# Layer 1's converted weights written over their raw high words, a PSUM bank of their own for the bits, and block 0's h in SBUF

## The chip, the cores and the metric

The kernel runs on one core of a Trainium2 chip. The metric is the device time of one execution in microseconds; the median of three runs of the kernel before is 961.95 us (960.44 to 962.39).

## What is computed

Strided and local attention over four batches of 576 tokens with eight heads, and then two dense feed-forward layers on all 2304 tokens. The weights come as float64. Cut to what matters:

```python
scores = scale * np.matmul(q, k.transpose(0, 1, 3, 2))
scores = np.where(masks[None, :, :, :], scores, -1000000000.0)
attn = np.exp(scores - np.max(scores, axis=-1, keepdims=True))
attn = attn / (np.sum(attn, axis=-1, keepdims=True) + 1e-09)
x = np.matmul(attn, v)            # then (2304, 512)
h = np.maximum(x @ w_in, 0.0)
x = h * h @ w_out                 # layer 1: 512 -> 2048 -> 512
h = x @ w_in2
P = a[0] + a[1] * h + a[2] * h**2 + a[3] * h**3
Q = 1.0 + np.abs(b[0]) * np.abs(h) + np.abs(b[1]) * h**2
out = (P / (Q + 1e-06)) @ w_out2  # layer 2
```

## The kernel before

The weights arrive as 64-bit floats, each as two 32-bit words. `to_f32` makes float32 of one half of a weight tile, 128 x 512 values: ACT takes the absolute value of the high word with a scale (L198, the tile `w32`, three buffers), VectorE shifts and masks it (L202), puts the sign in (L203) and the top bits of the low word (L204). For layer 1 the tile `bits` between these steps lies in PSUM, in the pool `psum` of eight banks that everything shares. `split_w` then rounds the float32 to fp32r for the high part `wh` (L220 on POOL, every fourth on ACT, L218) and subtracts for the low part `wl` (L221 on POOL, the first four on VectorE). A product of two float32 numbers is made of three fp32r matmuls: high by high, high by low, low by high.

The tokens are worked in six blocks of 384 (`NB`). A unit (j, f) of layer 1 is one of the 16 slices of 128 hidden columns for block j: `h_unit` runs 12 matmuls into one bank (L412), `act1` makes relu, square, the high part `gh` (L426) and the low part `gl` (L427), and `o_unit1`, two units later (`LAG`), runs 12 matmuls into the four banks of `acc` (L439). In block 0 h stays in its PSUM bank through all of `act1`: ACT does relu and square there, and VectorE makes `gl` from it. In later blocks relu goes to SBUF (L422), VectorE squares (L423) and POOL makes `gl`.

Attention runs in groups, two to a pair, woven into the units: scores (L285), maximum (L296), exponent (L309), row scale (L317, L318, L320), transposes (L327), values (L343), and the high and low parts of x (L368, L369). The groups of block 0 come first, then unit (0, 0) follows, and the groups of later blocks are spread over the units of the block before.

In block 0 the weights of layer 1 are converted just ahead of their use. `feed_w(3)` at the head of each unit converts three halves, in the order `wq`; 32 halves in all. The raw halves land in places that are free at that time (`homes`): the first 16 in tiles meant for later weights, the next 12 in eight of the same places again, and the last four in the staging pool; `load_raw` issues a load up to eight halves ahead, and a place that is used again waits until its earlier half has been read. In blocks 1 to 4 layer 2's weights are converted in the same way (`spill_w`) and written to DRAM.

The order of instructions on each engine is made by a scheduler at build time, by its own estimate of times and by the order in which the program text issues; at run time each engine keeps its order and waits on semaphores. TensorE, VectorE, ACT, POOL and the DMA queue of SP each have one.

Of the kernel before, what the change touches and what calls it, by code (L numbers as in the profile page):

```python
# [9 lines left out]
F32 = mybir.dt.float32  # L10
F32R = mybir.dt.float32r
I32 = mybir.dt.int32
BF16 = mybir.dt.bfloat16
AF = mybir.ActivationFunctionType
ALU = mybir.AluOpType
AX = mybir.AxisListType
PSUM = bass.MemoryType.PSUM

P = 128
# [3 lines left out]
DM, DFF = 512, 2048  # L23
NT = B * S
TB = 384
NB = NT // TB
NF = DFF // P
KT = DM // P
# [128 lines left out]
def moe_kernel(ctx, tc, qk, vp, w1, w2, a, b, masks, eye, out):  # L157
    nc = tc.nc
# [11 lines left out]
    gpool = ctx.enter_context(tc.tile_pool(name="gpool", bufs=1))  # L170
    first = ExitStack()
    stage = first.enter_context(tc.tile_pool(name="stage", bufs=3))
    psum = ctx.enter_context(tc.tile_pool(name="psum", bufs=8, space=PSUM))

    cst = cpool.tile([P, C_END], BF16, name="cst")
    ident = cpool.tile([P, P], F32, name="ident")
# [14 lines left out]
    def to_f32(layer, f, part, raw):  # L191

        lo, hi = raw[:, :, 0], raw[:, :, 1]
        w = stage.tile([P, DM], I32, tag="w32", bufs=3, name=f"w32_{layer}_{f}_{part}")
        wf = w.bitcast(F32)
        nc.scalar.activation(wf, hi.bitcast(F32), AF.Abs, scale=2.0**-112)  # L198
        bits = w
        if layer == 0:  # L200
            bits = psum.tile([P, DM], I32, tag="ps", name=f"bits{f}_{part}")
        nc.vector.tensor_scalar(bits, w, 3, 0x7FFFFFFF, ALU.logical_shift_left, ALU.bitwise_and)  # L202
        nc.vector.scalar_tensor_tensor(bits, hi, -0x80000000, bits, ALU.bitwise_and, ALU.bitwise_or)  # L203
        nc.vector.scalar_tensor_tensor(w, lo, 29, bits, ALU.logical_shift_right, ALU.bitwise_or)  # L204
        return wf

    def w_place(layer, f):
        wt[layer, f] = tuple(wpool.tile([P, 2 * DM], F32R, tag=f"w{c}{f}", name=f"w{c}{layer}_{f}") for c in "hl")
        return wt[layer, f]
# [3 lines left out]
    def split_w(wh, wl, wf):  # L213

        halves[0] += 1
        n = halves[0]
        if n % 4 == 0:
            nc.scalar.copy(wh, wf)  # L218
        else:
            nc.gpsimd.tensor_scalar(wh, wf, 1.0, 0.0, ALU.mult, ALU.add)  # L220
        (nc.vector if n <= 4 else nc.gpsimd).tensor_tensor(wl, wf, wh.bitcast(F32), ALU.subtract)  # L221
# [158 lines left out]
    def at_slot(n):  # L380

        load_groups(n + 4)
        if n < NG and n % 2 == 0:
            at_scores(n)
        if n < NG:
            at_max(n)
        if n == 2:
            warm_up(2)
        for m in range(max(0, n - 4), min(n, NG)):
            if n - m == lags(m)[1]:  # L390
                at_values(m)
        for m in range(max(0, n - 4), min(n, NG)):
            if n - m == lags(m)[0]:
                at_transpose(m)
        if n < NG:
            at_exp(n)
        for m in range(max(0, n - 4), min(n, NG)):
            if n - m == lags(m)[1]:
                at_out(m)
        if n < NG:  # L400
            at_norm(n)


    gt, acc = {}, {}

    def h_unit(layer, j, f, ps):
        xh, xl = xt[j]
        wh, wl = wt[layer, f]
        for kk in range(KT):
            c = slice(kk * P, (kk + 1) * P)  # L410
            for i, (w, x) in enumerate(((wh, xh), (wh, xl), (wl, xh))):
                nc.tensor.matmul(ps[:, :TB], w[:, c], x[:, kk, :], start=(kk == 0 and i == 0), stop=(kk == KT - 1 and i == 2))  # L412

    def act1(j, f, ps):
        psum_h = j == 0 or j == NB - 1 and f >= NF - EARLY
        if psum_h:
            nc.scalar.activation(ps[:, :TB], ps[:, :TB], AF.Relu)
            nc.scalar.activation(ps[:, :TB], ps[:, :TB], AF.Square)
            h = ps[:, :TB]
        else:  # L420
            h = gpool.tile([P, TB], F32, tag="r", name=f"r{j}_{f}", bufs=4)
            nc.scalar.activation(h, ps[:, :TB], AF.Relu)  # L422
            nc.vector.tensor_tensor(h, h, h, ALU.mult)  # L423
        gh = gpool.tile([P, TB], F32R, tag="gh", name=f"gh0_{j}_{f}", bufs=3)
        gl = gpool.tile([P, TB], F32R, tag="gl", name=f"gl0_{j}_{f}", bufs=3)
        last_act = nc.scalar.copy(gh, h).ins  # L426
        (nc.vector if psum_h else nc.gpsimd).tensor_tensor(gl, h, gh.bitcast(F32), ALU.subtract)  # L427
        gt[0, j, f] = gh, gl
        return last_act

    def o_unit1(j, f):
        if f == 0:
            acc[j] = [psum.tile([P, 512], F32, tag="ps", name=f"acc0_{j}_{e}") for e in range(KT)]
        gh, gl = gt.pop((0, j, f))
        wh, wl = wt[0, f]
        for e in range(KT):
            c = slice(DM + e * P, DM + (e + 1) * P)
            for i, (w, g) in enumerate(((wh, gh), (wh, gl), (wl, gh))):
                nc.tensor.matmul(acc[j][e][:, :TB], w[:, c], g, start=(f == 0 and i == 0), stop=(f == NF - 1 and i == 2))  # L439
# [39 lines left out]
    def load_raw(done):  # L479

        while len(raws) < min(len(wq), done + AHEAD):
            k = len(raws)
            place, free = homes[k]
            if slot < free or place and any(homes[i][0] == place for i in range(done, k)):
                break
            raws.append(load_w(0, *wq[k], place=place and "w" + place))
# [4 lines left out]
    def feed_w(n):  # L491
        for _ in range(n):
            load_raw(fed[0])
            if fed[0] < len(wq):
                f, part = wq[fed[0]]
                c = slice(part * DM, (part + 1) * DM)
                wh, wl = wt[0, f] if part else w_place(0, f)
                split_w(wh[:, c], wl[:, c], to_f32(0, f, part, raws[fed[0]]))
                fed[0] += 1
# [15 lines left out]
    def spill_w(f, part):  # L515

        wf = to_f32(1, f, part, load_w(1, f, part))
        parts = [stage.tile([P, DM], F32R, tag="w32", bufs=3, name=f"sp{c}{f}_{part}") for c in "hl"]
        split_w(*parts, wf)
        for z, t in enumerate(parts):  # L520
            nc.sync.dma_start(w2_dram[z, f][:, part * DM : (part + 1) * DM], t.bitcast(F32))
# [59 lines left out]
    NTT = TB // P  # L581

    def o_unit2(j, f):
        if f == 0:
            acc[1, j] = [psum.tile([P, 512], F32, tag="ps", name=f"acc1_{j}_{t}") for t in range(NTT)]
        gh, gl = gt.pop((1, j, f))
        wh, wl = wt[1, f]
        c = slice(DM, 2 * DM)
        pairs = ((gh, wh), (gh, wl), (gl, wh))
        for t, p in enumerate(acc[1, j]):  # L590
            for i, (g, w) in enumerate(pairs):
                nc.tensor.matmul(p, g[:, t * P : (t + 1) * P], w[:, c], start=(f == 0 and i == 0), stop=(f == NF - 1 and i == 2))  # L592
            if f == NF - 1:
                o = l2.tile([P, DM], F32, tag="osb", name=f"osb{j}_{t}", bufs=3)
                copy = nc.vector.tensor_copy if j == NB - 1 and t == 1 else nc.scalar.copy
                keep(copy(o, p))
                nc.sync.dma_start(out[j * TB + t * P : j * TB + (t + 1) * P, :], o)
# [18 lines left out]
    LAG2, EARLY = 6, 5  # L616
    ends = [slot, 23, 30, 38, 47, 51]
    spills = (0, 8, 16, 24, 2 * NF)
    for j, f in steps:
        if attn_open:  # L620
            goal, start_slot = ends[j + 1], ends[j]
            want = start_slot + -(-(goal - start_slot) * (f + 1) // (NF - 1))
            while slot < min(want, goal) or slot % 2 and slot < ends[-1]:
                at_slot(slot)
                slot += 1
            if slot >= ends[-1]:
                attn_open = False
        if j == 0:
            feed_w(3)
        ps = psum.tile([P, 512], F32, tag="ps", name=f"h0_{j}_{f}")  # L630
        h_unit(0, j, f, ps)
        last_act = act1(j, f, ps)
        if 0 < j < 5 and n2 < spills[j - 1] + -(-(spills[j] - spills[j - 1]) * (f + 1) // NF):
            with tc.issue_after(last_act):
                spill_w(n2 // 2, n2 % 2)
            n2 += 1
            if n2 == 2 * NF:
                first.close()
                l2 = ctx.enter_context(tc.tile_pool(name="l2", bufs=2))
        if j == NB - 1 and NF - EARLY > f >= NF - EARLY - KT:  # L640
            load_x1(0, f - (NF - EARLY - KT))
        prev.append((j, f))
        if len(prev) > LAG:
            finish(*prev.pop(0))
        if j == NB - 1 and f >= NF - EARLY:
            unit2(0, f - (NF - EARLY))
# [9 lines left out]
    for u in prev2:  # L656
        o_unit2(*u)
# [19 lines left out]
```

## Time and profile before

| | |
|---|---|
| median of three runs | 961.95 us |
| the profiled execution, and its span | 961.1 us, 959.3 us |
| TensorE matmuls busy | 902.9 us (94%) |
| VectorE, ACT, POOL busy | 672.0, 550.3, 592.2 us |
| mean granted TensorE clock | 0.974 of full speed |

Times in the views are microseconds from the start of the span. PE is TensorE, DVE VectorE, ACT ScalarE, POOL GpSimd, SP the engine that issues the DMAs. A row's "out<-in" names tiles by the program's names: `w` is the tile `w32`, `h` a PSUM bank of `h_unit`, `acc` an accumulator bank, `r` the SBUF tile of h. L198 is line 198 of the kernel. "Idle before" is the time in which the engine stood still just ahead of an instruction, and the arrow names what ended it.

### The profile page before, as it was taken

The numbers are of one execution on the slowest core, as the hardware profiler recorded it, in microseconds if no ns is written. First come the engines' busy times: TensorE is split into PE (matmuls) and PEld (weight loads), VectorE is DVE, ScalarE is ACT, GpSimd is POOL, SyncE is SP. The second block draws the span as 40 slices with busy tenths as digits, with TensorE's granted clock in tenths as the row PEclk, the third lists the DMA queues.
The fourth block names the chain that finished last, engine by engine and source line by source line (L and its number), as shares of the span: only waits on it lengthen the run. The fifth ranks groups of instructions, "written<-read, shape, count | busy, mean of one in ns | idle before, by whom it ended". The sixth has DMA issues, their size and how long they took to land.

```text
span 959.3 us, 14628 instructions
## 1 busy us (share of the span) xinstructions
PE 902.9 (94%) x5232; PEld 829.5 (86%) x5232; DVE 672.0 (70%) x792; ACT 550.3 (57%) x1391; POOL 592.2 (62%) x643
## 2 busy tenths in 40 slices
PE   6766589999999999999999999999999999999998
PEld 4555479999889989999999999999999989899896
DVE  3885752554644555544421469999999999999997
ACT  5654555444545445533323567777677777777774
POOL 3574751445445454544433368888888888887885
PEclk9777899999999999999999999999999999999999
DMA  8763330444453354343257550010010010000000
GB/s 294 265 214 116 117 117 29 138 138 149 158 172 123 117 164 158 99 150 115 78 180 277 205 203 18 9 42 17 9 50 9 9 51 9 9 33 1 33 1 33
DMA packets 40104, 98.55 MB, mean 103 GB/s; under 512 B 4704, under 2 KB 11616, under 8 KB 40032
## 3 DMA queue, kind: packets, MB, share of 16 engines
q1 hardware_dynamic: 40032, 97.62, 30.2%
q8 instruction: 41, 0.67, 0.3%
q14 instruction: 31, 0.25, 0.1%
HBM read 71.39 MB, written 26.21 MB: 102 GB/s over the span
## 4 chain that ended last, share of the span: by engine, by line
DVE 43%; PE 42%; ACT 5%; POOL 4%; issue 3%; DMA 2%; SPq 0%; POOLq 0%; ACTq 0%; DVEq 0%
DVE rq L559 23%; PE h L412 20%; PE acc L439 17%; DVE p L561 9%; DVE rq L570 7%; POOL wl L221 2%; PE ps_t L327 1%; PE ps_s L285 1%; PE ps_v L343 1%; ACT w L198 1%; DVE w L204 1%; DMA qk<-in_qk 1%; POOL wh L220 1%; DMA x_scratch<-x 1%; DVE r L423 1%
## 5 line engine op out<-in xcount | busy, mean ns | idle before, releaser
L412 PE MATMUL h<-xh,wh 128*128 128x384 f32 x768 | 260.9, 340 | 11.4 <-DVE w L204 10.2
L412 PE MATMUL h<-xh,wl 128*128 128x384 f32 x768 | 259.4, 338 | 0.0
L412 PE MATMUL h<-xl,wh 128*128 128x384 f32 x768 | 258.9, 337 | 0.0
L559 DVE RECIPROCAL rq<-w 128x384 f32<-128x384 f32 x96 | 243.9, 2541 | 17.2 <-POOL w L557 17.2
L412 PEld LDWEIGHTS h<-xh,wh 128*128 128x128 f32 x768 | 145.5, 189 | 18.5 <-DVE w L204 8.1
L412 PEld LDWEIGHTS h<-xl,wh 128*128 128x128 f32 x768 | 145.6, 190 | 3.8
L412 PEld LDWEIGHTS h<-xh,wl 128*128 128x128 f32 x768 | 145.3, 189 | 0.0
L427 POOL TENSOR_TENSOR gl<-r,gh 128x384 fp32r<-128x384 f32 x75 | 75.8, 1011 | 109.1 <-ACT gh L426 92.5
L578 POOL TENSOR_TENSOR gl<-rq,gh 128x384 fp32r<-128x384 f32 x96 | 115.1, 1199 | 39.8 <-ACT gh L577 39.8
L439 PE MATMUL acc<-gh,wh 128*128 128x384 f32 x384 | 130.3, 343 | 8.7 <-ACT gh L426 6.8
L439 PE MATMUL acc<-gl,wh 128*128 128x384 f32 x384 | 131.1, 341 | 0.0
L439 PE MATMUL acc<-gh,wl 128*128 128x384 f32 x384 | 130.4, 340 | 0.0
L423 DVE TENSOR_TENSOR r<-r 128x384 f32<-128x384 f32 x75 | 56.9, 758 | 104.0 <-ACT r L422 103.7
L557 POOL TENSOR_TENSOR w<-w,sq 128x384 f32<-128x384 f32 x96 | 97.5, 1016 | 46.6 <-ACT sq L554 46.6
L558 POOL TENSOR_TENSOR p<-p,hs 128x384 f32<-128x384 f32 x96 | 114.7, 1195 | 0.0
L592 PE MATMUL acc<-wh,gl 128*128 128x512 f32 x288 | 114.1, 396 | 0.3 <-POOL gl L578 0.3
L592 PE MATMUL acc<-wl,gh 128*128 128x512 f32 x288 | 113.7, 395 | 0.0
L592 PE MATMUL acc<-wh,gh 128*128 128x512 f32 x288 | 112.0, 389 | 0.0
L577 ACT CAST gh<-rq 128x384 fp32r<-128x384 f32 x96 | 49.4, 514 | 106.1 <-DVE rq L570 106.1
L561 DVE SCALAR_TENSOR_TENSOR p<-p,co,hs 128x384 f32<-128x384 f32 x96 | 99.2, 1033 | 0.0
L422 ACT ACTIVATE r<-h 128x384 f32<-128x384 f32 x75 | 36.8, 490 | 88.5 <-PE h L412 81.2
L439 PEld LDWEIGHTS acc<-gh,wh 128*128 128x128 f32 x384 | 72.4, 189 | 10.3 <-ACT gh L426 3.5
(74 smaller groups left out, 1549.4 us busy)
## 6 DMA issues: line engine op xcount, KB each, us to landing
wraw<-in_w SPq DMA_DIRECT2D x64, 512.0 KB, 4.3
w_scratch<-sph SPq DMA_DIRECT2D x32, 256.0 KB, 4.0
w_scratch<-spl SPq DMA_DIRECT2D x32, 256.0 KB, 3.2
wh<-w_scratch SPq DMA_DIRECT2D x16, 512.0 KB, 3.6
wl<-w_scratch SPq DMA_DIRECT2D x16, 512.0 KB, 4.5
v<-in_vp SPq DMA_DIRECT2D x24, 256.0 KB, 4.9
qk<-in_qk SPq DMA_DIRECT2D x12, 416.0 KB, 4.7
x_scratch<-x SPq DMA_DIRECT2D x24, 192.0 KB, 2.8
```

The lines of the kernel that those rows point to most:

```text
L412: nc.tensor.matmul(ps[:, :TB], w[:, c], x[:, kk, :], start=(kk == 0 and i == 0), stop=(kk == KT - 1 and i == 2))
L423: nc.vector.tensor_tensor(h, h, h, ALU.mult)
L427: (nc.vector if psum_h else nc.gpsimd).tensor_tensor(gl, h, gh.bitcast(F32), ALU.subtract)
L439: nc.tensor.matmul(acc[j][e][:, :TB], w[:, c], g, start=(f == 0 and i == 0), stop=(f == NF - 1 and i == 2))
L557: keep(nc.gpsimd.tensor_tensor(w, w, sq, ALU.add))
L558: keep(nc.gpsimd.tensor_tensor(p1, p1, hs, ALU.mult))
L559: keep(nc.vector.reciprocal(rq, w))
L561: keep(nc.vector.scalar_tensor_tensor(p1, p1, a1, hs, ALU.add, ALU.mult))
L570: keep(nc.vector.scalar_tensor_tensor(rq, p1, a0, rq, ALU.add, ALU.mult))
L577: keep(nc.scalar.copy(gh, rq))
L578: keep(nc.gpsimd.tensor_tensor(gl, rq, gh.bitcast(F32), ALU.subtract))
L592: nc.tensor.matmul(p, g[:, t * P : (t + 1) * P], w[:, c], start=(f == 0 and i == 0), stop=(f == NF - 1 and i == 2))
```

## The change

Layer 1's third conversion step writes into the raw tile, over its high words, so that `split_w` reads from there with a stride of two words, and `w32` is only read by the first step. `bits` has a pool of one bank (`psum_w`), and `psum` seven. In odd blocks of layer 1 and even blocks of layer 2 that bank serves as the first accumulator. In block 0 relu goes to the SBUF tile `r`, ACT squares it there, and VectorE's `gl` is issued at the head of the next unit, ahead of its conversions. `feed_w` converts two halves per unit.

```diff
--- before.py
+++ after.py
@@ -170,7 +170,8 @@
     gpool = ctx.enter_context(tc.tile_pool(name="gpool", bufs=1))
     first = ExitStack()
     stage = first.enter_context(tc.tile_pool(name="stage", bufs=3))
-    psum = ctx.enter_context(tc.tile_pool(name="psum", bufs=8, space=PSUM))
+    psum = ctx.enter_context(tc.tile_pool(name="psum", bufs=7, space=PSUM))
+    psum_w = ctx.enter_context(tc.tile_pool(name="psum_w", bufs=1, space=PSUM))
 
     cst = cpool.tile([P, C_END], BF16, name="cst")
     ident = cpool.tile([P, P], F32, name="ident")
@@ -194,15 +195,14 @@
 
         lo, hi = raw[:, :, 0], raw[:, :, 1]
         w = stage.tile([P, DM], I32, tag="w32", bufs=3, name=f"w32_{layer}_{f}_{part}")
-        wf = w.bitcast(F32)
-        nc.scalar.activation(wf, hi.bitcast(F32), AF.Abs, scale=2.0**-112)
-        bits = w
+        bits, to = w, w
         if layer == 0:
-            bits = psum.tile([P, DM], I32, tag="ps", name=f"bits{f}_{part}")
+            bits, to = psum_w.tile([P, DM], I32, tag="bits", name=f"bits{f}_{part}"), hi
+        nc.scalar.activation(w.bitcast(F32), hi.bitcast(F32), AF.Abs, scale=2.0**-112)
         nc.vector.tensor_scalar(bits, w, 3, 0x7FFFFFFF, ALU.logical_shift_left, ALU.bitwise_and)
         nc.vector.scalar_tensor_tensor(bits, hi, -0x80000000, bits, ALU.bitwise_and, ALU.bitwise_or)
-        nc.vector.scalar_tensor_tensor(w, lo, 29, bits, ALU.logical_shift_right, ALU.bitwise_or)
-        return wf
+        nc.vector.scalar_tensor_tensor(to, lo, 29, bits, ALU.logical_shift_right, ALU.bitwise_or)
+        return to.bitcast(F32)
 
     def w_place(layer, f):
         wt[layer, f] = tuple(wpool.tile([P, 2 * DM], F32R, tag=f"w{c}{f}", name=f"w{c}{layer}_{f}") for c in "hl")
@@ -401,7 +401,7 @@
             at_norm(n)
 
 
-    gt, acc = {}, {}
+    gt, acc, lows = {}, {}, []
 
     def h_unit(layer, j, f, ps):
         xh, xl = xt[j]
@@ -412,7 +412,7 @@
                 nc.tensor.matmul(ps[:, :TB], w[:, c], x[:, kk, :], start=(kk == 0 and i == 0), stop=(kk == KT - 1 and i == 2))
 
     def act1(j, f, ps):
-        psum_h = j == 0 or j == NB - 1 and f >= NF - EARLY
+        psum_h = j == NB - 1 and f >= NF - EARLY
         if psum_h:
             nc.scalar.activation(ps[:, :TB], ps[:, :TB], AF.Relu)
             nc.scalar.activation(ps[:, :TB], ps[:, :TB], AF.Square)
@@ -420,17 +420,30 @@
         else:
             h = gpool.tile([P, TB], F32, tag="r", name=f"r{j}_{f}", bufs=4)
             nc.scalar.activation(h, ps[:, :TB], AF.Relu)
-            nc.vector.tensor_tensor(h, h, h, ALU.mult)
+            if j == 0:
+                nc.scalar.activation(h, h, AF.Square)
+            else:
+                nc.vector.tensor_tensor(h, h, h, ALU.mult)
         gh = gpool.tile([P, TB], F32R, tag="gh", name=f"gh0_{j}_{f}", bufs=3)
         gl = gpool.tile([P, TB], F32R, tag="gl", name=f"gl0_{j}_{f}", bufs=3)
         last_act = nc.scalar.copy(gh, h).ins
-        (nc.vector if psum_h else nc.gpsimd).tensor_tensor(gl, h, gh.bitcast(F32), ALU.subtract)
+        low = lambda: (nc.vector if psum_h or j == 0 else nc.gpsimd).tensor_tensor(gl, h, gh.bitcast(F32), ALU.subtract)
+        if j == 0:
+            lows.append(low)
+        else:
+            low()
         gt[0, j, f] = gh, gl
         return last_act
 
+    def acc_bank(name, aside):
+
+        if aside:
+            return psum_w.tile([P, 512], F32, tag="bits", name=name)
+        return psum.tile([P, 512], F32, tag="ps", name=name)
+
     def o_unit1(j, f):
         if f == 0:
-            acc[j] = [psum.tile([P, 512], F32, tag="ps", name=f"acc0_{j}_{e}") for e in range(KT)]
+            acc[j] = [acc_bank(f"acc0_{j}_{e}", e == 0 and j % 2 == 1) for e in range(KT)]
         gh, gl = gt.pop((0, j, f))
         wh, wl = wt[0, f]
         for e in range(KT):
@@ -582,7 +595,7 @@
 
     def o_unit2(j, f):
         if f == 0:
-            acc[1, j] = [psum.tile([P, 512], F32, tag="ps", name=f"acc1_{j}_{t}") for t in range(NTT)]
+            acc[1, j] = [acc_bank(f"acc1_{j}_{t}", t == 0 and j % 2 == 0) for t in range(NTT)]
         gh, gl = gt.pop((1, j, f))
         wh, wl = wt[1, f]
         c = slice(DM, 2 * DM)
@@ -625,8 +638,10 @@
                 slot += 1
             if slot >= ends[-1]:
                 attn_open = False
+        while lows:
+            lows.pop()()
         if j == 0:
-            feed_w(3)
+            feed_w(2)
         ps = psum.tile([P, 512], F32, tag="ps", name=f"h0_{j}_{f}")
         h_unit(0, j, f, ps)
         last_act = act1(j, f, ps)

```

How the order moves at two places. The first is VectorE around the first low part of block 0. A name ends with its batch or block, its unit or half, and a build number: `wraw_5_0` is half 0 (the input weights) of slice 5, `gl_0_0` block 0's unit 0. Before:

```order
L204 SCALAR_TENSOR_TENSOR w_0_2_1_685<-wraw_2_1_364,bits_1_687 128x512
L204 SCALAR_TENSOR_TENSOR w_0_5_0_716<-wraw_5_0_440,bits_0_718 128x512
L202 TENSOR_SCALAR bits_1_728<-w_0_3_1_726 128x512
L203 SCALAR_TENSOR_TENSOR bits_1_728<-wraw_3_1_480,bits_1_728 128x512
L204 SCALAR_TENSOR_TENSOR w_0_3_1_726<-wraw_3_1_480,bits_1_728 128x512
L427 TENSOR_TENSOR gl_0_0_709<-h_0_0_693,gh_0_0_708 128x384
L202 TENSOR_SCALAR bits_0_738<-w_0_6_0_736 128x512
L202 TENSOR_SCALAR bits_1_765<-w_0_4_1_763 128x512
L203 SCALAR_TENSOR_TENSOR bits_0_738<-wraw_6_0_528,bits_0_738 128x512
```

After:

```order
L202 TENSOR_SCALAR bits_0_679<-w_0_4_0_678 128x512
L369 TENSOR_TENSOR xl_2_658<-ps_v_2_0_636,xh_2_657 128x12x14
L203 SCALAR_TENSOR_TENSOR bits_0_679<-wraw_4_0_365,bits_0_679 128x512
L430 TENSOR_TENSOR gl_0_0_703<-r_0_699,gh_0_0_702 128x384
L204 SCALAR_TENSOR_TENSOR wraw_4_0_365<-wraw_4_0_365,bits_0_679 128x512
L202 TENSOR_SCALAR bits_1_709<-w_0_2_1_708 128x512
L203 SCALAR_TENSOR_TENSOR bits_1_709<-wraw_2_1_367,bits_1_709 128x512
L430 TENSOR_TENSOR gl_0_1_745<-r_1_741,gh_0_1_744 128x384
L204 SCALAR_TENSOR_TENSOR wraw_2_1_367<-wraw_2_1_367,bits_1_709 128x512
```

Two halves were worked step by step in turn, each with its own bank, and `gl` stood behind ten converted halves with the next halves behind it. Now the steps of one half follow each other, `gl` stands between two of them, and it comes after six halves and two steps of the seventh.

The second is SP's queue at the loads of halves whose place is used again, with what each waits for. Before:

```order
L188 DMA wraw_10_1_916<-in_w 128x1024 [waits DMAHW5_49,DVE_49,Activation_49]
L188 DMA wraw_9_1_912<-in_w 128x1024 [waits DMAHW6_49,DVE_49,Activation_49]
L250 DMA qk_0_1_857<-in_qk 128x832 [waits DMAHW7_49,PE_49]
L253 DMA v_2_2_539<-in_vp 128x512 [waits DMAHW0_49,PE_49]
L188 DMA wraw_8_1_908<-in_w 128x1024 [waits DMAHW1_49,DVE_49,Activation_49]
L188 DMA wraw_7_1_904<-in_w 128x1024 [waits DMAHW2_49,DVE_49,Activation_49]
L188 DMA wraw_13_0_1026<-in_w 128x1024 [waits DMAHW3_49,DVE_49,Activation_49]
```

After:

```order
L189 DMA wraw_10_1_986<-in_w 128x1024 [waits DMAHW7_49,DVE_49,Pool_49]
L250 DMA qk_0_2_1066<-in_qk 128x832 [waits DMAHW0_49,PE_49]
L253 DMA v_0_0_625<-in_vp 128x512 [waits DMAHW1_49,PE_49]
L189 DMA wraw_9_1_982<-in_w 128x1024 [waits DMAHW2_49,DVE_49,Pool_49]
L189 DMA wraw_8_1_978<-in_w 128x1024 [waits DMAHW3_49,DVE_49,Pool_49]
L189 DMA wraw_7_1_974<-in_w 128x1024 [waits DMAHW4_49,Pool_49]
L250 DMA qk_0_0_1346<-in_qk 128x832 [waits DMAHW5_49,PE_49]
```

The loads waited for VectorE and ACT; now they wait for POOL, most of them for VectorE as well, and the loads of attention pairs stand at other places among them.

## Rows read from the trace of the kernel before

**Rows 1.** Busy us by engine, stretch by stretch (count), then clock, DMA share, GB/s.
```profile
54.00:80.00 26.00, 14.36 (x67) 12.44 (x68) 18.40 (x35) 13.94 (x33) 18.07 (x20) 0.70 0.59 201
80.00:104.00 24.00, 15.50 (x80) 14.13 (x81) 16.40 (x32) 9.62 (x26) 12.52 (x18) 0.86 0.16 50
104.00:136.00 32.00, 26.01 (x147) 22.98 (x148) 24.06 (x44) 18.36 (x51) 22.82 (x26) 0.89 0.45 147
136.00:176.00 40.00, 39.45 (x271) 37.38 (x268) 12.21 (x26) 20.95 (x68) 8.21 (x15) 1.00 0.14 43
```

**Rows 2.** Waits of PE, 176 to 552 us: total, times, longest.
```profile
PE ps_v L343 <- ACT at L335: 3.0, 3, 1.4
```

**Rows 3.** Waits of all engines, 54 to 136 us.
```profile
ACT w L198 <- POOL wl L221: 23.2, 17, 4.1
DVE gl L427 <- ACT gh L426: 11.0, 8, 4.7
PE h L412 <- DVE w L204: 10.2, 3, 7.0
...
DVE sm L318 <- POOL sm L317: 3.9, 3, 1.4
...
ACT w L198 <- DMA wraw<-in_w: 1.7, 1, 1.7
```

**Rows 4.** Chain that ended last, 85 to 180 us: start, length, what.
```profile
89.08 3.58 DMA wraw<-in_w
...
173.98 2.08 PE acc L439 x12
176.06 1.05 PE ps_s L285 x16
```

**Rows 5.** Groups by line, POOL, 20 to 140 us: busy, mean ns, idle before.
```profile
L221 POOL TENSOR_TENSOR wl<-w,wh 128x512 fp32r<-128x512 f32 x28 | 35.8, 1279 | 8.3 <-ACT wh L218 6.4
```

**Rows 6.** Timeline of DVE: start, length, what, idle before.
```profile
59.65 1.28 DVE L203 SCALAR_TENSOR_TENSOR bits<-wraw,bits 128x512 int32<-128x512 int32 x2
60.84 1.28 DVE L204 SCALAR_TENSOR_TENSOR w<-wraw,bits 128x512 int32<-128x512 int32 x2
62.03 0.69 DVE L202 TENSOR_SCALAR bits<-w 128x512 int32<-128x512 int32 x1
62.75 0.69 DVE L203 SCALAR_TENSOR_TENSOR bits<-wraw,bits 128x512 int32<-128x512 int32 x1
63.55 0.69 DVE L204 SCALAR_TENSOR_TENSOR w<-wraw,bits 128x512 int32<-128x512 int32 x1
64.94 0.56 DVE L427 TENSOR_TENSOR gl<-h,gh 128x384 fp32r<-128x384 f32 x1 [0.69 <-ACT gh L426]
```

**Rows 7.** Groups by line, ACT, 20 to 176 us.
```profile
L426 ACT CAST gh<-h 128x384 fp32r<-128x384 f32 x16 | 7.7, 479 | 0.4
```

**Rows 8.** Groups by line, DVE, 54 to 136 us.
```profile
L427 DVE TENSOR_TENSOR gl<-h,gh 128x384 fp32r<-128x384 f32 x9 | 5.0, 557 | 11.1 <-ACT gh L426 11.0
L369 DVE TENSOR_TENSOR xl<-ps_v,xh 128x84 fp32r<-128x84 f32 (+4 forms) x11 | 2.9, 267 | 1.6 <-ACT xh L368 1.6
L296 DVE TENSOR_REDUCE sm<-ps_s 72x2 f32<-72x144 f32 (+1 forms) x4 | 1.8, 485 | 0.0
L318 DVE RECIPROCAL sm<-sm 126x4 f32<-126x4 f32 (+2 forms) x6 | 1.0, 166 | 3.9 <-POOL sm L317 3.9
```

**Rows 9.** Groups by line, DVE, 176 to 560 us.
```profile
L423 DVE TENSOR_TENSOR r<-r 128x384 f32<-128x384 f32 x73 | 55.4, 759 | 101.2 <-ACT r L422 100.9
```

**Rows 10.** Timeline of DVE, 38 to 43 us.
```profile
39.02 1.52 DVE L221 TENSOR_TENSOR wl<-w,wh 128x512 fp32r<-128x512 f32 x1
...
42.61 0.69 DVE L221 TENSOR_TENSOR wl<-w,wh 128x512 fp32r<-128x512 f32 x1
```

**Rows 11.** Timeline of POOL, 38 to 43 us.
```profile
42.62 0.74 POOL L297 TENSOR_SCALAR sm<-sm 126x4 f32<-126x4 f32 x1
```

**Rows 12.** Timeline of PE at 54 us.
```profile
54.00 0.69 PE L412 MATMUL h<-xh,wh 128*128 128x384 f32 x1 [0.29 <-ACT e L309]
```

## The prediction

> **What bounds the kernel now.** I first read the busy time of each engine stretch by stretch [rows 1]. From 54 to 136 us, while block 0 of layer 1 runs its first units, TensorE is busy 14.36, 15.50 and 26.01 us, 55.9 of 82, and its granted clock averages 0.70, 0.86 and 0.89. From 136 to 176 it is busy 39.45 of 40 at clock 1.00. So 26 us of TensorE idle time and a slow clock lie in one place. After it TensorE has almost no slack: the largest wait between 176 and 552 us sums to 3.0 us [rows 2]. Layer 2 follows layer 1, so time saved in block 0 reaches the end unless something later gives it back. This is where the change lies.
>
> Next I read who waits for whom from 54 to 136 us [rows 3]. ACT's Abs (L198) waits 23.2 us in 17 waits for POOL's `wl` (L221): the buffer `w32`, of which there are three, is free only when the split of an older half is over. VectorE's `gl` (L427) waits 11.0 us for ACT's `gh`, and everything behind it on VectorE waits with it. TensorE then waits 10.2 us in three waits for a conversion (L204), 7.0 in the longest. Conversion is a ring through ACT, VectorE and POOL with three buffers; no engine in it is full (VectorE 18.40 + 16.40 + 24.06 = 58.9 of 82).
>
> The mark I count to is the end of block 0: its last output matmuls start at 173.98 and take 2.08, and 176.06 is the next attention pair [rows 4]. In both orders TensorE runs the same instructions up to there.
>
> **The change, part by part.**
>
> *The converted word goes over the raw high word.* Work: the same three VectorE steps per half; the write becomes strided. What moves is the buffer: `w32` is free after the first VectorE step, so the 23.2 us wait of Abs for POOL should go. The raw buffer is instead held until POOL's `wl` (1.279 us [rows 5]), and SP's later loads wait for POOL where they waited for VectorE and ACT, as the second place of the order shows. The one late load of before landed in 3.58 us [rows 4] and cost ACT 1.7 [rows 3]. Half (7,1) reuses the place of (6,1), and only half (9,0) and some attention steps stand between them on VectorE. After (6,1) come a cast, `wl` (together about 2 us), landing 3.6, issue and Abs about 1.5: 7 us, less about 2.2 for the half between. I charge 5 us, with 0 and 15 (three such reloads) as ends.
>
> *Bits get one bank.* Before, two halves alternated and four steps took 62.03 - 59.65 = 2.38 us, 0.60 each; a half alone has its steps 0.72 and 0.80 apart [rows 6]. With one bank every step hangs on the one before. In the changed order 76 steps remain from the first `gl` to the last conversion; 35 stand directly behind the previous step, 41 have something between. 35 x 0.76 + 41 x 0.60 = 51.2 us.
>
> *Block 0's h in SBUF.* ACT's relu and square read and write other memories; from PSUM each costs about what the cast beside them costs, 0.479 us [rows 7], and I keep that. The gain is that h leaves its bank after the relu. The low part is the cost: from PSUM `gl` takes 0.557 us [rows 8]; the nearest SBUF operation of the size, the square on VectorE in the later blocks, takes 0.759 [rows 9], both less 0.1 of overlap. `wl` on VectorE, also with two SBUF inputs, took 1.52 and 0.69 us in two neighbouring instances [rows 10], and beside the shorter POOL's small `sm` step lasted 0.74 [rows 11]. Scaled from 512 to 384 columns the dear one is 1.14. The ends are therefore 0.46 and 1.04 per `gl` after overlap; I take 0.66, by rows 9, the operation of the same size. 15 x 0.66 = 9.9 us (6.9 to 15.6).
>
> [...]
>
> *The low part one unit later, feed 2 in place of 3.* No work is added. `gl` of a unit is queued behind conversions of the next feed, so VectorE should find `gh` ready; the 11.0 us go. With 2 halves per unit VectorE's work per unit comes nearer to TensorE's two groups of 2.08.
>
> *Alternating accumulator bank.* Blocks 2 and 4 have three banks beside the accumulators for h and attention, where there were four. There are about six attention pairs in these blocks; the whole wait of TensorE today is 3.0 us of `at` [rows 2]. I charge 1.5 us, ends 0 and 24 (six times 4 us). Layer 2 has four or five banks for h in place of five and is paced by VectorE's chain; nothing is charged.
>
> **The sum.** VectorE is the engine that paces block 0 after the change. The first unit's matmul starts at 54.00 [rows 12]; its 12 matmuls take 3 us (between 2.08 and twice that), three ACT steps 1.5, an Abs between them 0.7: the first `gl` at about 59 (64.94 before [rows 6]). From there: 51.2 conversion + 9.9 lows + attention. Of attention 29 steps stand in that stretch; today's 21 take 2.9 + 1.8 + 1.0 = 5.7 us [rows 8], so 7.9. Together 69.0. Waits remain: the reciprocal waits for POOL 3.9 us over two pairs [rows 3], so 7.8 for four pairs, and the reload 5. The last conversion ends at 59 + 69.0 + 12.8 = 140.8. Behind it TensorE has five groups of 12 matmuls, 10.4 us, with the last low part 1.5: 152.7. Against 176.06 that saves 23.4 us; less 1.5 for the banks, 21.9. The profiled execution took 961.1 us (span 959.3), 0.85 under the median of the runs, 961.95. 961.1 - 21.9 = 939.2; as a median, **940 us**.
>
> Check against TensorE, which has its work to do anyway: 82 - 55.9 = 26.1 us idle, and of its busy time 14.36 x 0.30 + 15.50 x 0.14 + 26.01 x 0.11 = 9.3 us lies in the clock [rows 1]. Some 35.4 us is the most that can be saved, 926 us.
>
> **Range.** No waits and cheap lows (12.8 + 3.0) would give 924; TensorE's own work stops it at 926, the low end. Dear lows (+5.7) and two more late reloads (+10) give 956; 957 is the high end.
>
> **Rivals.**
>
> 1. *The low part is not late enough.* In the changed order the first `gl` stands between two steps of one half, and the next one three steps later; ACT's `gh` is an in-order step behind an Abs. For it: TensorE's clock is low there, so h comes late. Against: on average two halves, some 4 us, separate two `gl`. Then the 11.0 us of rows 3 stay: about 951. Chance 0.16, inside the range.
> 2. *A bank too few in blocks 2 and 4.* Six pairs at 4 us return 24 us: about 962, no change. For it: the changed order moves transposes behind eight more matmuls there. Against: other matmuls stand ready in the queue, and today's waits are near 1 us each. Chance 0.05.
> 3. *Reloads become the ring.* Twelve halves reuse a place. If each late one costs the 3.6 us of the load seen today, VectorE loses 43 us in place of the 5 charged: 940 + 38 = 978, slower. It decides from 2.3 us each: 12 x 2.3 = 27.6, which is the 5 charged and the 21.9 saved. For it: today one late load was followed by TensorE's 7.0 us wait. Against: most reused places lie three to four halves, 6 to 9 us, ahead of their use. Chance 0.09.
> 4. *More than forecast:* conversions also start earlier, beside attention, and unit 0 itself starts before 54 us, which moves TensorE's floor with it: under 926. Chance 0.06.
>
> The forecast has 0.64. About 0.2% is what a measurement of this kernel can tell from no change. Faster by more: 0.64 + 0.16 + 0.06 = 0.86; within it 0.05; slower 0.09. The range leaves out rivals 2, 3 and 4, 0.20.
>
> **What would show it.** Right: block 0's last output matmuls start near 150; Abs waits for POOL under 5 us in all; `gl` near 0.76 us, waiting little; TensorE's clock in 54 to 136 above 0.9; after block 0 the same distance to the end as before, within 3 us. Wrong: Abs waiting on loads several times (rival 3); `gl` waiting 10 us for `gh` (rival 1); TensorE waiting in blocks 2 and 4 (rival 2); or conversions ending before 128, in which case the price of the dependent steps was wrong.

## The result, and the profile after

Four runs of the changed kernel gave a median of 937.37 us (929.75 to 939.87), beside 962.17 us for the kernel before: a ratio of 0.9726, 95% interval 0.9702 to 0.975. The prediction was 940. The profiled execution has a span of 935.6 us, 23.7 less than before. The sum came out right, but two groups of its terms were wrong in opposite directions, and the part of the change that it counted as a cost brings most of the gain.

Busy time by engine, stretch by stretch, as in [rows 1]:

```profile
54.00:80.00 26.00, 23.64 (x165) 20.94 (x166) 24.39 (x46) 17.34 (x48) 19.54 (x25) 0.99 0.63 213
80.00:104.00 24.00, 22.00 (x137) 19.84 (x137) 18.71 (x35) 16.54 (x50) 15.45 (x20) 0.94 0.34 110
104.00:136.00 32.00, 29.28 (x173) 27.59 (x174) 24.84 (x42) 19.51 (x51) 22.43 (x26) 0.89 0.34 113
136.00:176.00 40.00, 40.00 (x277) 38.20 (x277) 21.64 (x39) 20.24 (x63) 20.38 (x26) 1.00 0.50 164
```

TensorE is busy 74.9 of the 82 us to 136, where it was busy 55.9, and its clock is 0.99 and 0.94 in the first two stretches, where it was 0.70 and 0.86; in the third it is 0.89, as before. The chain that ended last, at block 0's end, as in [rows 4]:

```profile
142.74 2.08 PE acc L452 x12
144.82 1.05 PE ps_s L285 x16
```

Block 0 ends at 144.82 us, 31.2 us earlier than at 176.06. The span is only 23.7 us shorter: from block 0's end to the program's end it took 783.2 us before and takes 790.8 now, so 7.6 us are given back.

Waits from 54 to 136 us, beside [rows 3]:

```profile
ACT w L201 <- DMA wraw<-in_w: 3.6, 3, 1.5
...
PE ps_t L327 <- DVE xl L369: 2.5, 1, 2.5
...
PE acc L452 <- POOL wl L221: 0.8, 1, 0.8
```

Abs waits no longer for POOL. It waits three times for a load, 3.6 us. No TensorE wait of this stretch names a conversion step of VectorE any more; one, of 0.8 us, is for POOL's `wl`.

VectorE from the first low part to the last conversion (53.14 to 136.15 us), by line:

```profile
L203 DVE SCALAR_TENSOR_TENSOR bits<-wraw,bits 128x512 int32<-128x512 int32 x26 | 17.9, 690 | 0.5
L204 DVE SCALAR_TENSOR_TENSOR wraw<-wraw,bits 128x512 int32<-128x512 int32 x26 | 17.8, 683 | 0.7
L202 DVE TENSOR_SCALAR bits<-w 128x512 int32<-128x512 int32 x25 | 17.2, 687 | 1.5 <-ACT w L201 1.2
L430 DVE TENSOR_TENSOR gl<-r,gh 128x384 fp32r<-128x384 f32 x15 | 12.8, 856 | 4.8 <-ACT gh L429 4.7
L296 DVE TENSOR_REDUCE sm<-ps_s 96x4 f32<-96x512 f32 (+1 forms) x8 | 4.6, 581 | 0.0
L369 DVE TENSOR_TENSOR xl<-ps_v,xh 128x84 fp32r<-128x84 f32 (+4 forms) x13 | 3.5, 266 | 3.3 <-ACT xh L368 3.3
L318 DVE RECIPROCAL sm<-sm 96x4 f32<-96x4 f32 (+1 forms) x8 | 1.3, 166 | 3.3 <-POOL sm L317 3.3
```

The idle times sum to 14.1 us of 83.0, which leaves 68.9 us for the work (the busy times sum to 75.1, since an instruction can start some 0.08 us before the one ahead of it ends: a `gl` at 68.54 behind a step of 0.69 us from 67.93). The prediction had 12.8 and 69.0.

### The profile page after: what moved, and what is told of

Same layout as the page of the kernel before. It is cut to its first block, busy times and chain, and to the rows that moved or that the text cites. A ratio compares the mean times of both kernels' runs of the same rounds, so it can differ in the third digit from the quotient of the medians.

```text
span 935.6 us, 14609 instructions
## 1 busy us (share of the span) xinstructions
PE 900.8 (96%) x5232; PEld 828.8 (89%) x5232; DVE 675.2 (72%) x792; ACT 550.7 (59%) x1391; POOL 595.5 (64%) x643
## 3 DMA queue, kind: packets, MB, share of 16 engines
q1 hardware_dynamic: 40032, 97.62, 31.2%
## 4 chain that ended last, share of the span: by engine, by line
DVE 42%; PE 39%; ACT 2%; POOL 2%; issue 1%; DMA 1%; SPq 0%; POOLq 0%; ACTq 0%
DVE rq L572 23%; PE h L412 19%; PE acc L452 16%; DVE p L574 9%; DVE rq L583 7%; PE ps_t L327 1%; PE ps_v L343 1%; POOL spl L221 1%; PE ps_s L285 1%; DMA x_scratch<-x 1%; DVE r L426 1%; PE acc L605 1%; ACT w L201 1%; DVE w L202 0%; DVE w L203 0%
## 5 line engine op out<-in xcount | busy, mean ns | idle before, releaser
L452 PE MATMUL acc<-gh,wh 128*128 128x384 f32 x384 | 132.2, 344 | 0.0
L426 DVE TENSOR_TENSOR r<-r 128x384 f32<-128x384 f32 x75 | 54.4, 726 | 107.0 <-ACT r L422 106.9
L590 ACT CAST gh<-rq 128x384 fp32r<-128x384 f32 x96 | 49.4, 514 | 106.1 <-DVE rq L583 106.1
L422 ACT ACTIVATE r<-h 128x384 f32<-128x384 f32 x91 | 44.7, 491 | 98.7 <-PE h L412 94.5
L429 ACT CAST gh<-r 128x384 fp32r<-128x384 f32 x91 | 46.8, 514 | 71.5 <-DVE r L426 71.1
```

Source lines behind the costliest of these rows:

```text
L590: keep(nc.scalar.copy(gh, rq))
```

## The experiments

Twelve kernels, each against the kernel before on the same chip. For each, the table gives the start of the third conversion step of the first half ("first"), of unit (0, 0), and of the third step of the last, 32nd half ("32nd"), the end of block 0 (the 192nd output matmul), and from there to the end of the span, all from one profiled execution, in us.

| kernel | first | unit 0 | 32nd | block 0 ends | rest | median of the runs |
|---|---|---|---|---|---|---|
| before | 31.2 | 54.0 | 132.7 | 176.1 | 783.2 | 962.2 |
| after | 23.6 | 47.8 | 135.5 | 144.8 | 790.8 | 937.4 |
| words_in_w32 | 22.4 | 48.9 | 141.9 | 152.3 | 787.9 | 942.4 |
| feed_three | 23.3 | 47.6 | 134.0 | 142.2 | 786.5 | 934.6 |
| low_at_once | 22.4 | 48.9 | 136.5 | 144.9 | 793.1 | 939.2 |
| h_in_psum | 24.3 | 48.6 | 134.8 | 143.7 | 788.6 | 934.1 |
| bits_common | 31.8 | 50.8 | 146.9 | 163.8 | 783.2 | 949.1 |
| aside_every | 24.3 | 49.4 | 136.5 | 144.8 | 786.4 | 933.0 |
| before_words | 31.0 | 53.4 | 133.8 | 178.2 | 783.2 | 963.3 |
| before_bank | 23.4 | 49.1 | 139.9 | 150.5 | 786.8 | 941.3 |
| before_bits_sbuf | 26.7 | 53.8 | 139.0 | 179.6 | 785.5 | 963.7 |
| bits_sbuf | 26.1 | 53.6 | 152.6 | 176.2 | 785.0 | 962.8 |
| every_three_psum | 24.6 | 49.6 | 135.5 | 145.7 | 786.2 | 934.4 |
| before_two_banks | 26.2 | 49.5 | 128.6 | 172.7 | 785.0 | 957.9 |

Read the fourth column against the fifth: the conversions end within 3 us of each other in the kernels before and after, and block 0 does not. Before, it ends 43 us behind the last conversion; now 9 us. The change did not make conversion faster; it let the units run beside it.

**One part undone at a time.** The words kept in w32:

```diff
-            bits, to = psum_w.tile(...), hi
+            bits = psum_w.tile(...)
```

> Theory A, the ring: writing the converted word over the high word is what freed Abs. With the word in the three w32 buffers again Abs waits for POOL's wl about 20 us, as it did before (23.2 us), and block 0 ends 15 to 20 us later: 952 to 957 us. Theory B, the order: in both profiles 32 halves take over 100 us from the first third step to the last (102 before, 113 after), so conversion was not made faster; the gain is that the units now run beside the conversions. Then the waits of Abs move the time by less than 5 us: 937 to 942.

Measured 942.35 us, ratio 0.9793 (0.9772 to 0.9814), just above theory B's bound. The ring is back, and block 0 ends 7.5 us later, not 15 to 20:

```profile
ACT w L201 <- POOL wl L221: 19.9, 17, 2.5
```

So 19.9 us of waits cost block 0 about a third of their length. The feed:

```diff
-            feed_w(2)
+            feed_w(3)
```

> Theory B, the order: with three halves ahead of each unit the low parts stand behind half again as many conversions and TensorE runs dry at the start of block 0, as it did before: 945 us or more. Theory A, the ring: VectorE has the same work in another order and the last conversion ends no later: 934 to 941.

Measured 934.64 us (0.9713, 0.9662 to 0.9764): within theory A's bounds; theory B in this form falls. Feed 2 brings nothing that shows. The late low part:

```diff
-        if j == 0:
-            lows.append(low)
-        else:
-            low()
+        low()
```

> The prediction's step: gl that is issued in its own unit waits for gh, 11.0 us in eight waits before, and all conversions behind it wait too: 945 to 950 us. Rival: with feed 2 and h in SBUF the scheduler finds a place for gl anyway, and the delay by a unit is worth under 3 us: 935 to 940.

Measured 939.17 us (0.9734, 0.9699 to 0.9768), block 0's end 144.9: the rival. The delay by a unit brings nothing that shows. And h in its bank:

```diff
-        psum_h = j == NB - 1 and f >= NF - EARLY
+        psum_h = j == 0 or j == NB - 1 and f >= NF - EARLY
```

> With h in its bank until the low part, one unit later, gl reads PSUM and costs 0.56 us for 0.89 (mean of the 16 in the profile after), so VectorE saves 5 us: if the price of gl decides, 931 to 934. If banks decide: three of seven are left beside the accumulators, h holds one for more than a unit, attention wants the others, and TensorE waits for banks: 942 to 950.

Measured 934.07 us (0.9704, 0.9688 to 0.9719), just above the first theory's bound. The low part costs 0.55 to 0.56 us from PSUM each time, but of the 5 us that VectorE was to save only 1.1 reach block 0's end. The second theory falls: moving h to SBUF brings nothing.

**The bank.** What is left is the pool of its own for `bits`. Undone in the changed kernel, with eight common banks and no accumulator aside:

```diff
-    psum = ctx.enter_context(tc.tile_pool(name="psum", bufs=7, space=PSUM))
-    psum_w = ctx.enter_context(tc.tile_pool(name="psum_w", bufs=1, space=PSUM))
+    psum = ctx.enter_context(tc.tile_pool(name="psum", bufs=8, space=PSUM))
...
-            bits, to = psum_w.tile([P, DM], I32, tag="bits", ...), hi
+            bits, to = psum.tile([P, DM], I32, tag="ps", ...), hi
...
-        if aside:
-            return psum_w.tile([P, 512], F32, tag="bits", name=name)
```

> Undoing the words, the feed, the late low part or h's place one at a time returned 7.5 us of block 0 at most, of the 31 that its end came earlier. Theory C, the bank: bits that take their turn in the common pool wait for banks that attention, h and the accumulators hold. Then block 0 ends 15 us later or more, unit 0 starts after 50 us again, and the time is 948 to 957. Theory D, no single part: any of them does most of it; then the time is 930 to 938, since blocks 2 and 4 get their fourth bank back.

Measured 949.12 us (0.9858, 0.9839 to 0.9876). Block 0 ends 19 us later; theory C. Then the same parts alone, in the kernel before. The words:

```diff
+        bits, to = w, w
...
+            to = hi
...
-        nc.vector.scalar_tensor_tensor(w, lo, 29, bits, ...)
-        return wf
+        nc.vector.scalar_tensor_tensor(to, lo, 29, bits, ...)
+        return to.bitcast(F32)
```

> The words over the high words alone, in the kernel before. The ring as the prediction had it: Abs loses its 23.2 us of waits for POOL and block 0 ends 7 us earlier or more: 950 to 955. Rival: VectorE's gl and the bank order hold the pace there, and the time is within 3 us of before: 959 to 963.

Measured 963.33 us (1.0004, 0.9989 to 1.0018): no change, at the upper edge of the rival's range. From 60 to 145 us Abs waits for loads in place of POOL. That is the mechanism of the prediction's rival 3, and it may be what takes back what the words bring; this run does not separate it from the wait for the bank, which is there as before:

```profile
ACT w L198 <- DMA wraw<-in_w: 14.0, 4, 6.4
...
PE h L412 <- DVE wraw L204: 7.7, 1, 7.7
```

The bank alone, with the alternating accumulator:

```diff
-    psum = ctx.enter_context(tc.tile_pool(name="psum", bufs=8, space=PSUM))
+    psum = ctx.enter_context(tc.tile_pool(name="psum", bufs=7, space=PSUM))
+    psum_w = ctx.enter_context(tc.tile_pool(name="psum_w", bufs=1, space=PSUM))
...
-            bits = psum.tile([P, DM], I32, tag="ps", ...)
+            bits = psum_w.tile([P, DM], I32, tag="bits", ...)
...
+            return psum_w.tile([P, 512], F32, tag="bits", name=name)
...
```

> The bank of bits and the alternating accumulator alone, in the kernel before. Theory C, the bank: the first third step comes near 24 us for 31, unit 0 starts before 50 us and the time is 945 to 953. The prediction's view, in which the one bank only costs: each step hangs on the one before, h holds its bank to the low part with one bank fewer in the pool, and the time is 962 to 972.

Measured 941.26 us (0.9771, 0.9754 to 0.9789), below theory C's range: some 21 of the 25 us, from this edit alone. Three readings show what it moves. First the start. ACT's Abs and VectorE's first step on it in the kernel before, then the first step in before_bank:

```profile
20.20 1.25 ACT L198 ACTIVATE w<-wraw 128x512 f32<-128x512 f32 x2
...
29.33 0.68 DVE L202 TENSOR_SCALAR bits<-w 128x512 int32<-128x512 int32 x1
```
```profile
20.44 0.69 DVE L203 TENSOR_SCALAR bits<-w 128x512 int32<-128x512 int32 x1
```

Before, the result of Abs lies there from 20.9 us, and the step is ordered 14 places further back on VectorE, among attention's steps. Second, TensorE's waits, 54 to 136 us. Before, beside the 10.2 us of [rows 3]:

```profile
PE ps_t L327 <- DVE gl L427: 4.5, 2, 4.3
PE ps_s L277 <- DVE w L204: 2.4, 1, 2.4
PE acc L439 <- DVE w L204: 1.8, 1, 1.8
```

L277 multiplies constants, and what it waits for can only be its bank, which `bits` holds until the third step. Weights come to TensorE from POOL or ACT (four low halves from VectorE's L221), never from L204, so the 10.2 us of `h` are bank waits as well, as far as its operands tell. `ps_t` waits for a bank that h holds until `gl`. In before_bank no wait of TensorE names the third step; the longest are:

```profile
PE ps_t L328 <- ACT e L310: 5.8, 3, 2.1
PE ps_v L344 <- DVE gl L428: 1.5, 3, 0.7
```

Third, ACT. With a bank for each of two halves the order put several Abs ahead of a unit's relu, and relu waited with them for the ring. Before:

```profile
75.18 0.67 ACT L198 ACTIVATE w<-wraw 128x512 f32<-128x512 f32 x1 [2.17 <-POOL wl L221]
77.11 0.66 ACT L198 ACTIVATE w<-wraw 128x512 f32<-128x512 f32 x1 [1.26 <-POOL wl L221]
77.68 0.47 ACT L417 ACTIVATE h<-h 128x384 f32<-128x384 f32 x1
```

That is the relu of unit 2, whose matmuls started at 62.26 and ended at 65.63. In before_bank it starts 3.3 us after its matmuls started (53.34), and in the changed kernel 2.3 us (54.38 after 52.10):

```profile
56.67 0.45 ACT L418 ACTIVATE h<-h 128x384 f32<-128x384 f32 x1
```

**Does any place of its own do?** The bits left in w32, in SBUF, with eight banks for all:

```diff
-            bits = psum.tile([P, DM], I32, tag="ps", ...)
```

> In the kernel before, the bits stay in w32 and take no PSUM bank; the pool keeps its eight. If it was the wait for a common bank that held conversion back, the first third step comes before 26 us, unit 0 before 50, and the time is 940 to 950. If it was the one bank that kept two halves from going abreast, and so let relu and gh pass ACT ahead of the next Abs, three buffers of w32 bring the old order back and the time is 955 to 965.

Measured 963.69 us (1.0017, 1.0006 to 1.0029). The same in the changed kernel, with eight common banks and no accumulator aside:

```diff
-            bits, to = psum_w.tile(...), hi
+            to = hi
```

> The changed kernel with the bits in w32, the converted word over the high word as now, eight common banks and no bank aside. If any place outside the common pool will do: block 0 ends within 3 us of 144.8, and blocks 2 and 4 have their four banks: 930 to 935. If the one bank's order counts: 940 to 950.

Measured 962.84 us (1.0002, 0.9993 to 1.0011); this misses both ranges. In before_bits_sbuf the time fell into the second range, but neither expectation had reckoned with the price of the steps. Groups of VectorE and POOL in bits_sbuf, 20 to 150 us (L202, L203 and L220 there are the steps L203, L204 and L221 of the changed kernel), and POOL's `wl` in the changed kernel:

```profile
L203 DVE SCALAR_TENSOR_TENSOR wraw<-wraw,w 128x512 int32<-128x512 int32 x31 | 32.0, 1039 | 0.3
L202 DVE SCALAR_TENSOR_TENSOR w<-wraw,w 128x512 int32<-128x512 int32 x31 | 27.6, 898 | 0.1
```
```profile
L220 POOL TENSOR_TENSOR wl<-wraw,wh 128x512 fp32r<-128x512 f32 x26 | 39.0, 1502 | 9.0 <-ACT wh L217 7.6
```
```profile
L221 POOL TENSOR_TENSOR wl<-wraw,wh 128x512 fp32r<-128x512 f32 x28 | 37.2, 1327 | 7.6 <-ACT wh L218 6.2
```

The two steps that now take both inputs from SBUF last 0.898 and 1.039 us where they lasted 0.690 and 0.683 (above), and POOL's `wl` 1.502 where it lasted 1.327. Over 32 halves that is 18 us of VectorE. Single steps of bits_sbuf last from 0.65 to 1.81 us. The changed kernel's trace shows what goes with such a length. Its layer 2 leaves the bits in w32: there the two steps last 0.67 to 0.69 us, and POOL works beside only two of the 64. The square of layer 1's later blocks (L426, in SBUF as well) lasts 0.54 to 0.56 us in the 38 cases in which POOL was idle the whole time; the 21 that last longer, 0.59 to 1.62, all lie beside POOL's work, and so do 16 of 0.55 or 0.56. With the bits in PSUM no L203 or L204 of layer 1 lasts over 0.70 us, though POOL works beside 29 and 24 of the 32. So the bits in PSUM also keep these two steps short. How much of the 25 us this price takes back is not shown: the order differs as well, and unit 0 starts at 53.6 us again.

Two banks of their own let two halves go abreast again. Against before_bank, with two accumulators of layer 1 aside from block 1 on:

```diff
-    psum = ... bufs=7 ...
-    psum_w = ... bufs=1 ...
+    psum = ... bufs=6 ...
+    psum_w = ... bufs=2 ...
```

> As before_bank (941.3 us), but bits has two banks of its own, the common pool six, and two accumulators of every block from block 1 on lie aside. Conversion starts as early as with one bank, but two halves may go abreast again, and in the changed order four Abs stand between gh of unit 2 and relu of unit 3 on ACT, as in the kernel before, where with one bank none to one does. If the early start is what the bank brings, block 0 ends within 4 us of before_bank: 938 to 946. If the order counts, that the units' relu does not stand behind Abs that wait: 950 to 960.

Measured 957.88 us (0.9943, 0.9924 to 0.9961). Unit 0 starts at 49.5 and the conversions end at 128.6, the earliest of all, and block 0 ends at 172.7. An early start and early conversions are not the gain by themselves. The time lies in the second range, but not for its reason: the relu of unit 3 starts at 88.30, as its matmuls end (88.21), and it is the matmuls that start late, at 84.0 where before_bank has 66.9. So the run doesn't settle that a single file of halves is what helps: two common banks were left beside the accumulators, and TensorE waited for one that h held until its low part (50 to 175 us):

```profile
PE ps_s L278 <- DVE gl L428: 7.1, 3, 4.0
```

How much of the bank's 21 us is the order and how much the banks that TensorE finds free stays open. For the changed kernel bits_common points to the order. There TensorE's waits that name the third step sum to 2.0 us from 54 to 136 us (three, the longest below), and block 0 still ends 19 us later; the longest are for work of ACT:

```profile
PE ps_v L342 <- ACT at L334: 8.5, 3, 3.5
PE acc L449 <- ACT gh L428: 4.8, 6, 2.6
PE h L411 <- ACT e L308: 2.9, 1, 2.9
PE ps_s L276 <- DVE wraw L203: 0.9, 1, 0.9
```

**What is given back later.** The bank lies idle in blocks 2 and 4. Here an accumulator lies in it in every block, first and last of the four in turn:

```diff
-acc_bank(f"acc0_{j}_{e}", e == 0 and j % 2 == 1)
+acc_bank(f"acc0_{j}_{e}", j > 0 and e == (0 if j % 2 else KT - 1))
...
-acc_bank(f"acc1_{j}_{t}", t == 0 and j % 2 == 0)
+acc_bank(f"acc1_{j}_{t}", t == (NTT - 1 if j % 2 else 0))
```

> The order is the changed kernel's to the middle of block 2; from there blocks 2 and 4 have four banks beside the accumulators again. Theory, a bank too few: the stretch of 29.3 us in block 2 (clock 0.88) takes 24.4 again at clock 1.00, as before; the distance from block 0's end to the end of the span is 784 to 786 us for 790.8: 930 to 933. Rival: the clock falls there for another reason (the phase between conversion and attention), and the time stays at 936 to 938.

Measured 933.02 us (0.9686, 0.9671 to 0.9701), the lowest median, and 786.4 us from block 0's end: the theory, with both figures just above its bounds. One stretch between two attention pairs in block 2, as windows: of the changed kernel, of the kernel before, of aside_every.

```profile
271.07:300.38 29.31, 26.85 (x157) 25.48 (x156) 12.56 (x24) 11.60 (x35) 12.48 (x16) 0.88 0.34 101
```
```profile
301.64:325.99 24.35, 23.98 (x157) 22.77 (x156) 13.01 (x23) 10.73 (x34) 12.61 (x16) 1.00 0.37 111
```
```profile
269.80:294.10 24.30, 23.93 (x157) 22.76 (x156) 12.98 (x23) 10.74 (x34) 12.59 (x16) 1.00 0.36 109
```

The loss of 5.0 us is 2.1 of idle time (29.31 - 26.85 against 24.35 - 23.98) and 2.9 of slower matmuls. With three banks the pair's first transpose stands behind ten output matmuls and waits for the bank that `xl` frees, and the values that follow it wait too. The two in the changed kernel; then both transposes of the pair before, where the first follows an earlier group's values at once and only the second waits:

```profile
276.15 0.52 PE L327 MATMUL ps_t<-ident,e 96*128 96x96 f32 x4 [1.72 <-DVE xl L369]
...
278.15 0.91 PE L343 MATMUL ps_v<-at,v 128*64 128x96 f32 x8 [0.74 <-ACT at L335]
```
```profile
302.99 0.55 PE L327 MATMUL ps_t<-ident,e 96*128 96x96 f32 x4
...
305.67 0.55 PE L327 MATMUL ps_t<-ident,e 96*128 96x96 f32 x4 [0.37 <-DVE xl L369]
```

The waits are the order's, but the clock is not: h_in_psum and feed_three have the same two waits (1.74 and 0.75 us), and in their profiled executions the clock stays at 1.00 and the stretch takes 26.66 and 26.64 us. In h_in_psum:

```profile
269.97:296.63 26.66, 24.18 (x157) 22.80 (x157) 12.58 (x24) 11.62 (x35) 12.52 (x16) 1.00 0.36 111
```
```profile
275.07 0.52 PE L327 MATMUL ps_t<-ident,e 96*128 96x96 f32 x4 [1.74 <-DVE xl L369]
...
277.07 0.55 PE L343 MATMUL ps_v<-at,v 128*64 128x96 f32 x8 [0.75 <-ACT at L335]
```

So the missing bank costs some 2.3 us here each time (26.66 against 24.35), and the clock 2.7 more in some executions. With feed_three, whose clock does not fall, the rest after block 0 takes 786.5 us, as little as in aside_every; with bits_common, which has eight common banks, 783.2, as before.

The two stretches after this one, 300.38 to 335.00 us in the changed kernel, take 34.62 us for 32.68, at clock 0.91 in the second (316.32 to 335.00); in aside_every 32.7. aside_every loses 3.8 us in layer 2 instead, from the first output matmul there to the last 392.9 us for 389.1, as the bank that it uses again there is still being emptied:

```profile
PE acc L605 <- ACT osb L609: 5.4, 3, 2.3
```

Layer 1's half of this edit without layer 2's was not tried. The last run joins aside_every, feed 3 and h in PSUM:

```diff
-            feed_w(2)
+            feed_w(3)
...
-        psum_h = j == NB - 1 and f >= NF - EARLY
+        psum_h = j == 0 or j == NB - 1 and f >= NF - EARLY
```

> The bank aside in every block (933.0 by itself), three halves ahead of a unit (block 0 ended 2.6 us earlier by itself) and h of block 0 in PSUM to its late low part (1.2 us earlier). If they add: 928 to 930. If the clock and the banks take it back: 932 to 936.

Measured 934.39 us (0.972, 0.9705 to 0.9736): they don't add. Block 0 ends at 145.7, later than with feed 3 (142.2) or h in PSUM (143.7) alone.

## Why the prediction was right, and where it was not

The forecast for the profiled execution was 939.2 us; it took 937.4 (961.1 - 23.7). Step by step:

- **The first low part at 59.** It came at 53.14, 5.9 us earlier. The prediction started its count at the 54.00 of [rows 12], as if conversion began when it did before. This was the mechanism of rival 4, with its chance of 0.06.
- **From there to the last conversion, 81.8.** Measured 83.0: work 68.9 for 69.0, waits 14.1 for 12.8. The price of the dependent steps held. The low part cost 0.856 for 0.759; 15 of them at 0.1 of overlap make 11.3 us for 9.9. The reloads cost VectorE at most 1.2 us (its wait for Abs), not 5. `gl` waited 4.7 us for `gh`, under half of what rival 1 had; issued at once, in low_at_once, it waited 4.7 as well (45 to 145 us).
- **The tail, 11.9.** Measured 8.7 (136.15 to 144.82). These three terms put block 0's end at 144.8, not 152.7.
- **The banks in blocks 2 and 4, 1.5.** Measured 7.6 over the whole rest in this execution, 5.0 of it in one pair. The mechanism was rival 2's; the step that failed is its price, which was taken from waits alone. They came to more than 1.5 (2.3 in that pair), and here the clock fell behind them as well. Without such a fall, in feed_three, the whole rest lost 3.2 us (786.47 against 783.25).
- **What brings the gain.** This failed outright. "What moves is the buffer" gave it to the 23.2 us of Abs; that wait went, and it is worth 7.5 us of block 0 in the changed kernel and nothing in the kernel before. The bank of bits stands in the sum as a cost alone, the price of dependent steps. The misread row was "PE h <- DVE w" in [rows 3], taken for a wait for the converted weights. By its operands it was a wait for a bank, and so pointed at the part that decides.
- **Two SBUF inputs** were weighed for the low part, which lasted 0.54 to 0.56 us seven times and 0.98 to 1.36 nine times: its 11.3 us lie between the two sums, 9.9 and 15.6. They matter more where the prediction did not look, in the conversion steps once the bits lie in SBUF. The long ones each lay beside POOL's `wl` for 0.57 us or more, the short ones for 0.44 at most. The short ones are no shorter than those from PSUM in h_in_psum (0.55 to 0.56).

Of the prediction's own signs, two came true: Abs waits for POOL no longer, and `gl` waits little. Three did not: the last output matmuls of block 0 start at 142.74, not near 150; `gl` takes 0.856, not 0.76; and the distance to the end grew by 7.6 us where 3 were allowed. The clock from 54 to 136 us is above 0.9 in two stretches of the three.

The size came out right in part since pacing by VectorE, the count of its steps and their prices were right. The rest is luck: 7.9 us too few saved by block 0's end and 6.1 too few given back after it nearly cancel, and more than half of what was given back depends on the execution. The fastest of the four runs, 929.75 us, lies inside the range, but 10 us from the forecast.

## What to carry to other kernels

When two engines share a pool of PSUM banks, read a wait on the other engine's last step as a possible wait for the bank; operands that only come from elsewhere give it away, as in the 10.2 us of [rows 3]. A scratch tile with a bank of its own costs a bank and can still win: here it brought some 21 of the 25 us, as it takes one producer out of the order in which all others get theirs, and it changes the order that the scheduler makes. Price a new wait of TensorE with and without a fall of the clock behind it (here 5.0 us and 2.3), and look at more than one execution. Give an idle bank a second use in every phase, but not one whose last reader is still at work, which cost 5.4 us of waits in layer 2 of aside_every.

## What the runs showed of the hardware

TensorE stood still twice before a slow piece, for 1.72 us and then 0.74. In windows of 2 us of the changed kernel the granted clock then falls to 0.50 of full speed:

```profile
274.00:276.00 2.00, 0.43 (x3) 0.11 (x1) 2.00 (x6) 0.18 (x1) 1.17 (x2) 1.00 0.47 134
276.00:278.00 2.00, 1.25 (x8) 0.96 (x8) 1.29 (x3) 1.08 (x6) 1.09 (x3) 0.88 0.55 208
278.00:280.00 2.00, 1.85 (x12) 1.53 (x13) 0.18 (x1) 1.49 (x9) 0.82 (x2) 0.50 0.96 247
```

It stays at 0.50 to 284 us, although TensorE is busy without a break from 280. Before, with 0.37 us of idle time in the whole stretch, it stays at 1.00. But the same two stops do not always bring the fall. Six kernels have them in block 2 (1.72 to 2.02 us, then 0.74 or 0.75): in one profiled execution of each, the clock falls there in three (after, low_at_once, words_in_w32; means over the span 0.982, 0.980 and 0.980) and stays at 1.00 in three (feed_three, h_in_psum, before_bank; 0.993, 0.989 and 0.987). In the eight others, which do not have them, it falls nowhere in block 2; in the stretches above it is 1.00 in the kernel before and in aside_every.

The runs show the same. The four of the changed kernel have mean clocks of 0.982, 0.994, 0.980 and 0.982 and took 937.38, 929.75, 937.35 and 939.87 us: the one with the higher clock is 7.6 us faster than the next. The five of aside_every, without the stops, have 0.989 to 0.991 and lie within 2.4 us. What decides in which execution the clock falls was not shown.
